# Storing V's projected memory rows by pairs of head rounds, a gate moved behind its block's projections, and another order inside a segment of a memory-recurrent attention kernel

## The chip, the cores and the metric

The kernel runs on one core of a Trainium2 chip. The metric is the time of one execution on the device in microseconds (us), the median of several. The engines are named as in the profile: PE multiplies matrices (PEld loads its weights), DVE, ACT and POOL compute on vectors, SP only issues DMAs; ACT issues DMAs too. PE writes to PSUM, and DVE or ACT copies from there to SBUF.

## The reference

Two attentions over the same x (2048 x 640, bf16) are mixed by a gate. A is a recurrence over 64 segments of 32 tokens with 8 memory tokens in front; the memory of a segment is part of the output of the one before. B is a local dilated attention. A has 32 heads of 192, so its three projections and its output projection are 640 x 6144 each.

```python
for s in range(n_seg):                       # 64 segments of 32 tokens
    h = jnp.concatenate([mem, xs], axis=1)   # 8 + 32 tokens
    q, k, v = h @ Wq, h @ Wk, h @ Wv         # per head
    scores = jnp.where(mask, q @ k.T * scale, -1e9)
    o = einsum(softmax(scores) @ v, Wo)
    mem = o[:, :M]; outs.append(o[:, M:])
g = sigmoid((x * gate_w).sum(-1))
return g * a + (1 - g) * b
```

## The kernel before, in words

The kernel has four stages. **Part B** (`part_b`) computes the local attention in blocks of 512 tokens, the gate and the transposed x. Its order per engine is set by a scheduler that starts from the order of the program. **The prepass** (`prepass`) computes q, k and v of the last 8 tokens of each segment for all 64 segments at once and stores them in DRAM, as zqk and zv. **The recurrence** (`part_a`) then needs, per segment, the projections of the 32 rows (8 memory, 24 tokens) in `hT`, and loads the other 8 tokens' rows from DRAM. **Part z** makes the outputs of those last 8 tokens after the recurrence. From the prepass on, each engine does its instructions in exactly the order of the program.

The 32 heads are taken in four rounds R of 8 (a round is a slice of 1536 columns), and the rounds in two halves h. A weight slice is 128 x 1536 bf16, 384 KB; there are 80, of which 67 lie in SBUF and 13 are streamed from DRAM in each segment, through four buffers `wst`, by SP (`load_slice`, L401 for the input weights, L400 for copies of Wo). SP issues a streamed load once its buffer is free.

One segment goes, on PE: `m_qk(0, ...)` (L580) projects q and k of the first half into the first two of four PSUM bank pairs, `m_qk(1, ...)` those of the second half into the other two; `m_qk`'s argument lists the chunks of 128 of the model width, and the last chunk is followed by `copy_pair` (L588), one copy on ACT (0.80 us) and one on DVE (0.96 us). `t_qk(h)` transposes a half (twelve 128 x 128 transposes, L607, three at a time, to the bank pairs that the copies have just read) and copies the result (L610 on DVE, L611 on ACT). `s_a`, `s_b` make the scores (L626, L635), `e_exp` the exponentials (L643, ACT) and two masks (L646, L648, DVE), `e_sum` the sums (L653, L655, PE) and their reciprocals (ACT), `e_norm` multiplies; `m_v` projects v, `pv_half` (L682, L686) multiplies with v, `o_group` (L716) is the output projection, `sel` (L729) and `tail` (L808) make the next memory and the output. In the first half, before: chunk 0 of `m_qk(1)`, `t_qk(0)`, the load of zv (`load_vz`, L566, ACT's queue), chunks 1 and 2, the scores and exponentials, chunks 3 and 4, `m_v(0, (0, 1))`, the loads of a4 (L759) and hT (L559) on ACT's queue, `t_qk(1)`, `e_sum(0)`.

V's prepass takes the rounds in the order 1, 3, 2, 0. In a round, four tiles of 128 rows (16 segments x 8 tokens) are projected (15 matmuls, L492) into one of two PSUM tiles, copied by ACT and DVE in turn (L80, L82) into one of four buffers of `zv4`, and stored by four DMAs of SP (L499), one for each of the four head groups j, in runs of 384 elements (768 bytes). Between the rounds stand loads of weights: `begin` (streamed slices ahead of time) and `load_late` (L415, slices that stay, into space that has become free). The rows of a segment's zv are the keys in the order j, round, token; `maskB`, built by POOL in `build_sel` (L522, L525, L528), says which of these keys belong to a query's round.

In part B, `make_xT(b)` transposes a block of x (L172), then computes the block's gate: twenty matmuls of one column (L183) with the gate's weight gw, an exponential on ACT (L186), three small operations on DVE (L187 to L189); then POOL makes the copies xh and zT (L193, L194, L197). `make_v` (L222) and `proj` (L235) follow, and a loop over 40 steps of scores, values and outputs. The loads are issued in the order x, mem, wv, the raw q and k weights, gw (L146).

Of the kernel before, what the change touches and what calls it, by code (L numbers as in the profile page):

```python
# [7 lines left out]
ACT = mybir.ActivationFunctionType  # L8
ALU = mybir.AluOpType
AX = mybir.AxisListType  # L10
BF = mybir.dt.bfloat16
F32 = mybir.dt.float32
# [33 lines left out]
class _K:  # L46
# [51 lines left out]
    def part_b(self):  # L98

        nc, tc, KC, S = self.nc, self.tc, self.KC, self.S  # L100
        NQ, HALO = 121, 14
# [9 lines left out]
        with ExitStack() as ctx:  # L111
# [55 lines left out]
            def make_xT(b):  # L167
# [11 lines left out]
                ps_g = bank(F32, "ps_g")  # L179
                for i in range(4):  # L180
                    c0 = HALO + t0 + 128 * i
                    for kc in range(KC):
                        nc.tensor.matmul(ps_g[:, i:i + 1], lhsT=xT[:, kc, c0:c0 + 128], rhs=gw[:, kc, :],  # L183
                                         start=(kc == 0), stop=(kc == KC - 1), skip_group_check=True)
                gs = slice(4 * b, 4 * b + 4)
                nc.scalar.activation(gz[:, gs], ps_g[:, 0:4], ACT.Exp, scale=-1.0)  # L186
                nc.vector.tensor_scalar_add(gz[:, gs], gz[:, gs], 1.0)  # L187
                nc.vector.reciprocal(self.g_sb[:, gs], gz[:, gs])
                nc.vector.tensor_scalar(out=self.omg_sb[:, gs], in0=self.g_sb[:, gs], scalar1=-1.0, scalar2=1.0,  # L189
                                        op0=ALU.mult, op1=ALU.add)  # L190
# [12 lines left out]
            nc.vector.tensor_copy(self.memT[:], ps[:, 0:8 * KC].rearrange("p (c i) -> p c i", i=8))  # L203

# [103 lines left out]
            proj(*steps[0])  # L308
            nc.gpsimd.memset(wop[:], 0.0)
# [4 lines left out]
            for i, (b, g) in enumerate(steps):  # L314
                if g == 2 and b + 1 < S // 512:
                    make_xT(b + 1)
                if (b, g) == (S // 512 - 1, 0):
# [111 lines left out]
    def prepass(self):  # L429
# [3 lines left out]
        NZ = nseg * 8  # L433
# [10 lines left out]
        with tc.tile_pool(name="pre_ps", bufs=1, space=bass.MemoryType.PSUM, reuse_waits="tile") as psp:  # L444
            n = 1
            for m in "qk":
                for R in range(4):
                    ZS2 = zs2[:, R // 2, :].rearrange("p (s f) -> p s f", f=192)
                    ZS = ZS2[:, :, 96 * (R % 2):96 * (R % 2) + 96]
                    if (m, R) == ("k", 2):  # L450
                        self.begin(*streamed("k", 2, 3), *streamed("v", 1), *streamed("v", 3)[0:1])
# [3 lines left out]
                    for t in range(3):  # L455
# [9 lines left out]
                        else:  # L465
                            dst = ZS.rearrange("p s (i c) -> p s i c", c=12)[:, :, :, 4 * t:4 * t + 4]
# [6 lines left out]
            for x, R in enumerate((1, 3, 2, 0)):  # L473
                sls = [self.get_slice(("v", R, kc)) for kc in range(KC)]
                if x == 1:
                    self.begin(*streamed("v", 2))
                if x == 2:
# [5 lines left out]
                    self.begin(*streamed("k", 0, 1))  # L483
                if x == 3:
                    self.begin(*streamed("k", 2, 3))
                for st in range(NZ // 128):
                    i = 4 * x + st
                    ZV = zv4[:, 1536 * (i % 4):1536 * (i % 4) + 1536]
                    ps = psp.tile([128, 4, NZ], F32, name=f"ps_pre{n % 2}")
                    for kc in range(KC):  # L490
                        for g in range(3):
                            nc.tensor.matmul(ps[:, g, :], lhsT=zT[:, kc, 128 * st:128 * st + 128],  # L492
                                             rhs=sls[kc][:, 512 * g:512 * g + 512], start=(kc == 0),
                                             stop=(kc == KC - 1))
                    self.evac(ZV.rearrange("p (g f) -> p g f", g=3), ps[:, 0:3, :], "act" if n % 2 else "dve")
                    n += 1
                    dst = self.zv_dram[16 * st:16 * st + 16].rearrange("s (j r i) f -> s j r i f", j=4, r=4)
                    for j in range(4):
                        nc.sync.dma_start(dst[:, j, R], ZV[:, 384 * j:384 * j + 384])  # L499
# [433 lines left out]
```

## Time and profile before

| | |
|---|---|
| time, median of 3 runs (lowest to highest) | 1759.71 us (1758.57 to 1762.41) |
| the profiled execution | 1759.71 us, of which the span from first to last instruction 1758.0 us |
| instructions | 80093 |
| PE busy | 1624.2 us, 92% of the span |
| ACT, DVE, POOL busy | 685.7, 641.9, 31.9 us |
| DMA | 434.53 MB, mean 247 GB/s |
| mean granted PE clock | 0.988 |

In the profile's lines, L12 is line 12 of the kernel. A line of a timeline has the start in us from the span's start, the length in us, the engine, the line, the operation, what it writes <- reads, the shapes and the count of merged instructions; brackets hold the idle time of the engine before it and what ended it. SPq and ACTq are the sequencers of SP and ACT, which issue the DMAs. `ps_d_5092` and `ps_d_5093` are the PSUM bank pairs of the first half, `ps_d_5090` and `ps_d_5091` those of the second; `zv_4165` is zv4, `zs_4166` the buffer zs2. A busy PE isn't PE at its peak, since the ends of matmuls are modelled; the starts are what the steps below are read from.

### The profile page before, as it was taken

Reading aid. Unit: us, or ns where it says so; the run is one execution under the profiler, and the core shown is the slowest. Engines: PE = TensorE matmul, PEld = TensorE weight load, DVE = VectorE, ACT = ScalarE, POOL = GpSimd, SP = SyncE. Lnnn points to the kernel's source line nnn. Section 1 sums busy time; section 2 is a strip of 40 time slices with the busy share of each in tenths; the row PEclk is TensorE's granted clock in tenths of the full one; section 3 lists DMA queues with packets and bytes.
Section 4 is the critical chain, followed back from the end, with each engine's and each line's share of the span. In section 5 each row is a group of like instructions: output and inputs, shape, how many; then the busy total and the mean of one; then the engine's idle time right before and its main releaser. Section 6 shows DMA issues by size and latency. Waiting matters only on the chain.

```text
span 1758.0 us, 80093 instructions
## 1 busy us (share of the span) xinstructions
PE 1624.2 (92%) x42085; PEld 751.7 (43%) x30693; DVE 641.9 (37%) x1542; ACT 685.7 (39%) x1372; POOL 31.9 (2%) x70
## 2 busy tenths in 40 slices
PE   7998999977999999999999999999999999999989
PEld 4555544433334334434444334444434444344447
DVE  4655522223333333333333333333333333333321
ACT  4766622213333333333343333443333443334340
POOL 5100000000000000000000000000000000000000
PEclk9999999989999999999999999999999999999989
DMA  9310195878888888898888988988988998989881
GB/s 331 82 29 17 42 309 142 230 228 272 282 280 278 281 280 280 278 297 274 281 286 276 285 272 274 290 284 281 292 273 280 293 286 273 294 282 290 278 269 31
DMA packets 264299, 434.53 MB, mean 247 GB/s; under 512 B 88845, under 2 KB 149781, under 8 KB 263957
## 3 DMA queue, kind: packets, MB, share of 16 engines
q1 hardware_dynamic: 172744, 378.52, 67.1%
q10 hardware_dynamic: 91212, 50.87, 10.6%
q8 instruction: 285, 4.67, 1.0%
q14 instruction: 58, 0.47, 0.1%
HBM read 395.62 MB, written 34.86 MB: 245 GB/s over the span
## 4 chain that ended last, share of the span: by engine, by line
PE 67%; DMA 10%; ACT 8%; DVE 7%; issue 4%; SPq 2%; ACTq 1%; DVEq 0%
PE ps_d_5093 L580 9%; PE ps_d_5091 L580 9%; DVE ZQKV L588 6%; DMA wst<-in_A_Wv_dram 6%; PE ps_d_5092 L716 6%; PE ps_d_5093 L716 6%; PE ps_d_5092 L580 6%; PE ps_d_5090 L580 5%; PE ps_bqk L235 3%; ACT ZQKV L693 3%; ACT bP L258 2%; PE ps_d_5093 L865 2%; PE ps_d_5093 L607 2%; PE ps_d_5091 L607 1%; PE ps_d_5091 L865 1%
## 5 line engine op out<-in xcount | busy, mean ns | idle before, releaser
L580 PEld LDWEIGHTS <-hT 128*32 128x32 bf16 x5632 | 155.3, 96 | 342.1 <-issue 258.2
L588 DVE CAST ZQKV<-ps_d_5093 128x768 bf16<-128x768 f32 x128 | 122.6, 958 | 206.3 <-PE ps_d_5093 L580 206.3
L716 PEld LDWEIGHTS <-ZQKV 128*32 128x32 bf16 x4608 | 124.2, 96 | 115.4 <-ACT ZQKV L693 55.6
L607 PEld LDWEIGHTS <-ZQKV 128*128 128x128 bf16 x1536 | 91.5, 98 | 123.5 <-ACT ZQKV L588 84.5
L716 PE MATMUL ps_d_5093<-zs_4166,ZQKV 128*32 128x384 bf16 x1792 | 140.0, 330 | 2.2 <-issue 2.2
L716 PE MATMUL ps_d_5092<-zs_4166,ZQKV 128*32 128x256 bf16 x2304 | 131.6, 277 | 7.7 <-issue 2.3
L588 ACT CAST ZQKV<-ps_d_5092 128x768 bf16<-128x768 f32 x64 | 51.2, 800 | 188.1 <-PE ps_d_5092 L580 188.1
L580 PE MATMUL ps_d_5091<-wst,hT 128*32 128x384 bf16 x1280 | 109.1, 329 | 7.5 <-DMA wst<-in_A_Wv_dram 3.1
L580 PE MATMUL ps_d_5093<-wst,hT 128*32 128x384 bf16 x1024 | 89.2, 328 | 15.2 <-DMA wst<-in_A_Wv_dram 14.7
L611 ACT COPY ZQKV<-ps_d_5091 128x768 bf16<-128x768 bf16 x64 | 51.1, 799 | 85.7 <-PE ps_d_5091 L607 81.1
L611 ACT COPY ZQKV<-ps_d_5093 128x768 bf16<-128x768 bf16 x64 | 51.1, 799 | 83.3 <-PE ps_d_5093 L607 83.3
L693 DVE CAST ZQKV<-ps_d_5091 128x384 bf16<-128x384 f32 x64 | 35.7, 558 | 117.6 <-PE ps_d_5091 L686 117.6
L626 PEld LDWEIGHTS <-ZQKV 128*32 128x32 bf16 (+1 forms) x4096 | 50.2, 92 | 65.2 <-ACT ZQKV L611 50.7
L716 PE MATMUL ps_d_5093<-zv_4165,ZQKV 128*32 128x384 bf16 x1024 | 71.9, 325 | 6.1 <-issue 5.9
L588 DVE CAST ZQKV<-ps_d_5091 128x768 bf16<-128x768 f32 x64 | 61.3, 958 | 38.8 <-PE ps_d_5091 L580 38.8
L646 DVE TENSOR_TENSOR ZQKV<-ZQKV,maskA 128x160 bf16<-128x160 bf16 x128 | 30.6, 239 | 122.6 <-ACT ZQKV L643 122.6
L716 PE MATMUL ps_d_5092<-wst,ZQKV 128*32 128x256 bf16 x768 | 71.8, 278 | 2.2 <-issue 2.2
L588 ACT CAST ZQKV<-ps_d_5090 128x768 bf16<-128x768 f32 x64 | 51.2, 799 | 45.7 <-PE ps_d_5090 L580 44.8
L258 ACT ACTIVATE bP<-ps_bS 128x968 bf16<-128x968 f32 (+1 forms) x80 | 64.7, 855 | 4.6 <-PE ps_bS L253 3.8
L682 PEld LDWEIGHTS <-ZQKV 32*128 32x128 bf16 (+1 forms) x4096 | 43.1, 97 | 49.7 <-ACT ZQKV L588 24.4
L693 ACT CAST ZQKV<-ps_d_5090 128x384 bf16<-128x384 f32 x64 | 30.7, 479 | 82.2 <-PE ps_d_5091 L686 79.9
L693 DVE CAST ZQKV<-ps_d_5093 128x384 bf16<-128x384 f32 x64 | 35.7, 558 | 67.9 <-PE ps_d_5093 L686 67.9
(639 smaller groups left out, 3849.8 us busy)
## 6 DMA issues: line engine op xcount, KB each, us to landing
wst<-in_A_Wk_dram SPq DMA_DIRECT2D x260, 384.0 KB
wst<-in_A_Wv_dram SPq DMA_DIRECT2D x260, 384.0 KB
wst<-wscr SPq DMA_DIRECT2D x192, 384.0 KB
wst<-in_A_Wq_dram SPq DMA_DIRECT2D x130, 384.0 KB
zqk_dram<-zs_4166 ACTq DMA_DIRECT2D x4, 3072.0 KB
ZQKV<-zqk_dram ACTq DMA_DIRECT2D x64, 192.0 KB
zv_dram<-zv_4165 SPq DMA_DIRECT2D x64, 96.0 KB
ZQKV<-zv_dram ACTq DMA_DIRECT2D x64, 96.0 KB
```

The costliest lines, as they stand in the source:

```text
L235: nc.tensor.matmul(ps[:, 0:nn], lhsT=wqk[n][:, kc, 4 * g:4 * g + 4, :].rearrange("p h d -> p (h d)"), rhs=xT[:, kc, o0:o0 + nn], start=(kc ...
L258: nc.scalar.activation(Pv, ps[0:nk, :, 0:nq * nu], ACT.Exp, scale=scale_b)
L580: mm = nc.tensor.matmul(dst[x // 2][32 * j:32 * j + 32, x % 2, 0:384], lhsT=hT[:, kc, :], rhs=sl[:, 384 * j:384 * j + 384], start=(kc == 0 ...
L588: cp(KV[:, 384 * u:384 * u + 768].rearrange("p (a f) -> p a f", a=2), ps[:, :, 0:384])
L607: nc.tensor.transpose(p[:, r, t, :], unit[2 * r + m][:, 128 * t:128 * t + 128], self.ident[:])
L611: nc.scalar.copy(KV[:, 4 * 384:6 * 384].rearrange("p (c b i) -> p c b i", b=4, i=8), blocks(pk))
L626: nc.tensor.matmul(pSs[h][32 * j:32 * j + 32, par, 40 * r:40 * r + 40], lhsT=KT[R][k0:k1, c, :], rhs=q_blocks(R)[k0:k1, :, c, :], start=(r ...
L646: nc.vector.tensor_tensor(out=EA, in0=EA, in1=self.maskA[:].unsqueeze(1).unsqueeze(1).to_broadcast([128, 2, 2, 40]), op=ALU.mult)
L682: nc.tensor.matmul(out[:, r, t, :], lhsT=V[2 * h + r][ks, f0:f1], rhs=E[ks, par, 40 * r:40 * r + 40], start=(r == 0 and t == 0), stop=Fals ...
L693: cp(oTxs[2 * h + jp].rearrange("p (j c) q -> p j c q", j=2), src[:, :, :, 8:40])
L716: mm = nc.tensor.matmul(b_out[part][32 * jj:32 * jj + 32, 0:n], lhsT=oTxs[2 * (R // 2) + j // 2][:, 6 * (j % 2) + 3 * (R % 2) + t, :], rhs ...
L865: nc.tensor.matmul(ps[32 * q:32 * q + 32, 0:nf], lhsT=oz[n, q][:, 24 * (R // 2) + 6 * j + 3 * (R % 2) + t, :], rhs=wo[part, c // nc_][:, c ...
```

## The change

Three things are changed.

*Part B.* The gate moves out of `make_xT` into a function `make_g`. For block 0 it is called behind `make_v(0)` and the first `proj`, for the others right behind `make_xT`, where it was, but with POOL's copies ahead of it in the program.

*The prepass.* V's rounds are taken in pairs, (0, 1) and then (2, 3). For a tile of rows both rounds are projected, copied into one of two buffers of twice the size, and stored by four DMAs with runs of 768 elements (1536 bytes): 32 DMAs in place of 64. For this the keys of a pair are interleaved (j, pair, token, round), k's in the same manner, and `maskB` is built for that order, with one select by POOL in place of three per head group, and seven additions and a copy on DVE. The loads between the rounds move to the two pairs.

*The segment.* `m_qk(1)` does chunks 0 and 1 before `t_qk(0)`, and 2, 3 and 4 behind it, all of them before the first half's scores.

```diff
@@ part_b: the gate's lines move from make_xT to a function of their own @@
+            def make_g(b):
+                t0 = 512 * b
                 ps_g = bank(F32, "ps_g")
...
             make_v(0)
             proj(*steps[0])
+            make_g(0)
             nc.gpsimd.memset(wop[:], 0.0)
...
                     make_xT(b + 1)
+                    make_g(b + 1)
@@ prepass, k's part @@
-                        self.begin(*streamed("k", 2, 3), *streamed("v", 1), *streamed("v", 3)[0:1])
+                        self.begin(*streamed("k", 2, 3), *streamed("v", 1))
...
-                            dst = ZS.rearrange("p s (i c) -> p s i c", c=12)[:, :, :, 4 * t:4 * t + 4]
+                            dst = ZS2.rearrange("p s (i r c) -> p s i r c", r=2, c=12)[:, :, :, R % 2, 4 * t:4 * t + 4]
@@ prepass, v's part @@
-            for x, R in enumerate((1, 3, 2, 0)):
-                sls = [self.get_slice(("v", R, kc)) for kc in range(KC)]
-                if x == 1:
-                    self.begin(*streamed("v", 2))
-                if x == 2:
+            for rp in range(2):
+                Rs = (2 * rp, 2 * rp + 1)
+                sls = {R: [self.get_slice(("v", R, kc)) for kc in range(KC)] for R in Rs}
+                if rp == 0:
+                    self.begin(*streamed("v", 2), *streamed("v", 3))
+                else:
                     self.load_late(2, slices(zs2[:, 1, :]))
                     nc.scalar.dma_start(self.ZQKV[:, 608:1376], self.zqk_dram[0])
...
-                    self.begin(*streamed("k", 0, 1))
-                if x == 3:
-                    self.begin(*streamed("k", 2, 3))
+                    self.begin(*streamed("k", 0, 1)[0:2])
                 for st in range(NZ // 128):
-                    i = 4 * x + st
-                    ZV = zv4[:, 1536 * (i % 4):1536 * (i % 4) + 1536]
...
+                    ZV = zv4[:, 3072 * (st % 2):3072 * (st % 2) + 3072].rearrange("p (j r f) -> p j r f", j=4, r=2)
+                    for R in Rs:
+                        ps = psp.tile([128, 4, NZ], F32, name=f"ps_pre{n % 2}")
...
+                        self.evac(ZV[:, :, R % 2, :], ps[:].rearrange("p g n -> p (g n)")[:, 0:1536].rearrange(
+                            "p (j f) -> p j f", j=4), "act" if n % 2 else "dve")
+                        n += 1
+                    if (rp, st) == (1, NZ // 128 - 1):
+                        self.begin(*streamed("k", 0, 1)[2:3], *streamed("k", 2, 3))
+                    dst = self.zv_dram[16 * st:16 * st + 16].rearrange("s (j a i r) f -> s j a i (r f)", j=4, a=2, r=2)
                     for j in range(4):
-                        nc.sync.dma_start(dst[:, j, R], ZV[:, 384 * j:384 * j + 384])
+                        nc.sync.dma_start(dst[:, j, rp], ZV[:, j].rearrange("p r f -> p (r f)"))
@@ build_sel @@
-            mb = self.maskB[sl, :, :]
...
+            nc.gpsimd.affine_select(out=self.maskB[sl, :, 0:8].rearrange("p (a r) i -> p a r i", r=2),
+                                    in_=ones[sl, 0:32].rearrange("p (a r i) -> p a r i", a=2, r=2),
+                                    pattern=[[-16, 2], [-1, 2], [-2, 8]], compare_op=ALU.is_equal, fill=0.0, base=0,
                                     channel_multiplier=1)
...
+        for q in range(1, 8):
+            nc.vector.tensor_add(self.maskB[:, :, q], self.maskB[:, :, q - 1], self.maskB[:, :, q])
+        nc.vector.tensor_copy(self.maskB[:, :, 8:16], self.maskB[:, :, 7:8].to_broadcast([128, 4, 8]))
@@ part_a, one segment @@
-                m_qk(1, (0,))
+                m_qk(1, (0, 1))
                 t_qk(0)
                 load_vz(s)
-                m_qk(1, (1, 2))
+                m_qk(1, (2, 3, 4))
                 for chunks in (FULL, HALF):
                     s_a(0, chunks)
                     s_a(1, chunks)
                     s_b(0, chunks)
                 e_exp(0)
-                m_qk(1, (3, 4))
                 if s == 0:
                     self.load_late(3, self.last_tiles)
                 m_v(0, (0, 1))
```

## The prediction

> **What bounds the kernel.** I read the page first, then the busy time by stage, then the order of work on PE, DVE and SP in one segment and in the V prepass. The page's chain of waits is mostly matmuls:
>
> ```profile
> PE 67%; DMA 10%; ACT 8%; DVE 7%; issue 4%; SPq 2%; ACTq 1%; DVEq 0%
> ```
>
> PE holds two thirds of the chain, so time is won only where PE stands still. By stage (start:end, length, busy time of each engine, granted clock, DMA share, GB/s):
>
> ```profile
> 0.00:223.00 223.00, 193.98 (x2729) 114.73 (x2729) 117.65 (x227) 142.20 (x256) 31.93 (x70) 0.98 0.31 99
> 327.00:392.00 65.00, 54.28 (x242) 23.85 (x241) 16.53 (x10) 11.51 (x8) 0.00 (x0) 0.92 0.85 233
> 392.00:421.00 29.00, 21.07 (x576) 8.87 (x393) 6.92 (x18) 7.78 (x17) 0.00 (x0) 0.88 0.83 252
> 421.00:1692.00 1271.00, 1192.08 (x36368) 511.61 (x25190) 464.57 (x1254) 487.63 (x1065) 0.00 (x0) 0.99 0.89 283
> ```
>
> The last row is 63 of the 64 segments of the recurrence, 20.2 us each; the third is the first segment, 8 us longer; the second is the V prepass, PE idle for some 11 of 65 us. All three parts of the change fall into these rows: the order inside a segment counts 64 times, the rest once.
>
> **Part 1, the order inside a segment.** The change does 32 instead of 16 matmuls between the last projection of the first half and its transposes (t_qk(0), L607), and does all of m_qk(1) before the first half's scores. PE, one segment, before:
>
> ```profile
> 1011.36 0.34 PE L580 MATMUL ps_d_5091<-wlate_k_0_4119,hT 128*32 128x384 bf16 x4
> 1011.63 0.34 PE L607 MATMUL ps_d_5092<-ident,ZQKV 128*128 128x128 bf16 x3
> 1012.15 0.33 PE L607 MATMUL ps_d_5093<-ident,ZQKV 128*128 128x128 bf16 x3 [0.18 <-DVE ZQKV L588]
> 1012.32 0.33 PE L607 MATMUL ps_d_5092<-ident,ZQKV 128*128 128x128 bf16 x3
> ...
> 1016.71 0.34 PE L607 MATMUL ps_d_5090<-ident,ZQKV 128*128 128x128 bf16 x3
> 1017.13 0.33 PE L607 MATMUL ps_d_5091<-ident,ZQKV 128*128 128x128 bf16 x3
> 1017.30 0.33 PE L607 MATMUL ps_d_5090<-ident,ZQKV 128*128 128x128 bf16 x3
> ...
> 1017.63 0.23 PE L653 MATMUL ps_d_5092<-ZQKV,bones 128*128 128x160 bf16 x1
> ```
>
> Three transposes take 0.165 us (1012.15 to 1012.32), but the second three of each half start 0.52 and 0.42 us after the first. They overwrite the bank pair that DVE is still copying:
>
> ```profile
> 1011.14 0.96 DVE L588 CAST ZQKV<-ps_d_5093 128x768 bf16<-128x768 f32 x1 [2.20 <-PE ps_d_5093 L580]
> ...
> 1015.34 0.19 DVE L648 TENSOR_TENSOR ZQKV<-ZQKV,maskB 128x64 bf16<-128x64 bf16 x1
> 1016.12 0.96 DVE L588 CAST ZQKV<-ps_d_5091 128x768 bf16<-128x768 f32 x1 [0.60 <-PE ps_d_5091 L580]
> ```
>
> The first copy ends at 1012.10 and the transposes go on at 1012.15; the second ends at 1017.08 and they go on at 1017.13. So PE loses 0.52 - 0.165 = 0.355 and 0.42 - 0.165 = 0.255, together 0.61 us a segment; the list of waits has the first 63 times.
>
> After: call T the end of m_qk(1). Eight groups of four take 1.31 us (1014.60 to 1015.91), so t_qk(0) starts 0.65 us later than now, at 1012.28, after the copy. t_qk(1) now comes behind the scores (0.55) and 16 matmuls of V (0.65, plus 0.1 to 0.15 to change over), at T+1.30. DVE's copy starts at T+0.21 and ends at T+1.17. Both waits go. Number of matmuls, loads and changes of shape: the same.
>
> What is late next is the softmax of the first half. Now its masks end at 1015.53 and the sums on PE (L653) start at 1017.63: 2.10 us of slack. The change takes from it the 1.31 us of matmuls that move ahead and the 0.255 us of the lost wait; and the masks stand behind DVE's copy, so they start at T+1.18, not at 1.13 us (1014.05 to 1015.18) after the scores' start: 0.05. That leaves 0.48 us. On ACT the copy of the first bank pair runs from T-0.06 to T+0.74, and exp could start at T+0.74 anyhow, so it isn't held. Behind exp in ACT's queue stand the loads of a4 and hT (issue 0.55 and 0.49 us), then the copy of t_qk(1)'s K (L611): they are out by about T+1.9, L611 is due at T+2.2; 0.3 us to spare. The wait that the page lists for exp, DMA ZQKV<-zv_dram in 37 segments, I don't believe: in the timeline exp starts 0.12 us after PE's last score ends. SP's streamed weights keep their order; the tightest lead, V's first slice, falls from 5.3 us (issue 1011.08, use 1016.40) to about 4.9.
>
> So 0.61 us, if nothing is given back. Something will be: DMA is at 0.89 of its time and 20.2 us become 19.6, so 0.92, and PE stalls on "issue" for 4% of the chain, 70 us or 1.1 us a segment:
>
> ```profile
> 1022.59 0.20 PE L686 MATMUL ps_d_5093<-ZQKV 32*64 32x32 bf16 x2 [1.30 <-issue]
> ```
>
> The same instructions from the first half's scores to the second half's now stand in 4.76 us (1014.05 to 1018.81) and will stand in 3.2. I let the stalls grow by a tenth, 0.11 us; the ends are nothing and a third (0.36). Net 0.50 us x 64 = **32 us** (16 to 39). The Trainium skill (Runtime: NRT & Kernel Launch, Instruction fetch mechanics) has the sequencer fetch the next block of instructions while the present one runs, a crossing "mostly hidden". By it I would give back nothing and arrive some 7 us lower; the row of 1.30 us says otherwise, if that stall is a fetch.
>
> **Part 2, V's prepass.** Its 16 tiles of 15 matmuls take 3.24 us each (333.61 to 336.85), 51.8 us; from 327.14 to 392.02 are 64.9. The rest stands in two rows of PE, and what SP did meanwhile says why:
>
> ```profile
> 381.80 1.44 PE L492 MATMUL ps_pre_5044<-wlate_v_0_4127,ZQKV 128*128 128x512 bf16 x3 [8.76 <-ACT zv_4165 L80]
> 392.02 0.35 PE L580 MATMUL ps_d_5092<-wres_q_0_71,hT 128*32 128x384 bf16 x4 [1.85 <-DVE zv_4165 L82]
> ```
> ```profile
> 362.62 7.67 SPq L415 DMA_DIRECT2D zs_4166<-in_A_Wo_dram  x8
> 370.39 3.08 SPq L401 DMA_DIRECT2D wst<-in_A_Wk_dram  x3
> 373.56 11.25 SPq L499 DMA_DIRECT2D zv_dram<-zv_4165  x16
> ```
>
> SP issues a store each 0.64 us, without a pause from 346 to 396; ACT can't empty PSUM into zv4 before the stores of the round before have landed, and PE waits 8.9 us (372.88 to 381.80), runs the next tile at half the clock (1.7 us more) and ends 2.0 us late. While SP issues the last sixteen (385 to 396) DMA is busy for 0.67: the issue is the limit, not the bytes. The change makes 32 stores of twice the size. That one takes as long to issue is not shown for stores; the weight loads, four times as large in as many rows, take 0.33 to 0.53 us to issue while the queue has room. So I take 0.64; the other end is 1.28. Half of the issues, 32 x 0.64 = 20 us, leave SP. Walked through: first pair's last stores out by 358, eight weights by 365, two streamed weights by 367, first stores of the second pair 367 to 369.6, landed some 3.3 us later (as the lane that a store of 352.35 frees at 355.68), 372.9, where tile buffer 0 is wanted at 369.5; PE loses 2 us, ends at 381 and hands over at 383 instead of 392: **9 us** (0 with 1.28 us an issue; 10 at best). The interleaved keys cost PE and DVE nothing there: the same copies in another order, masks built elsewhere.
>
> The first segment waits 1.72 us for a q and 5.86 us for a v slice, both behind the last stores in SP's queue. These end 2.6 instead of 4.0 us into the segment, with fewer packets pending: **2.5 us** (0 to 6). The Trainium skill (DMA: Bandwidth & Descriptors, Specifications) puts the shortest transfer at full rate at 512 bytes. That speaks against this part: 768 bytes are above it already, and by bytes alone I would leave out the 9 us and forecast some 9 us more. The 0.67 while SP issues decides for me.
>
> **Part 3, the gate.**
>
> ```profile
> 14.32 0.69 PE L183 MATMUL ps_g<-gw_sb,xT 128*128 128x1 bf16 x20 [5.45 <-DMA gw_sb<-in_gate_w_dram]
> 14.87 8.15 PE L222 MATMUL ps_bv<-wv_sb,xT 128*128 128x320 bf16 x40
> ```
>
> V's projections stand behind a gate that waits for its weight. x's last copy ends at 9.62; wv is issued before raws that land by 11.04; so L222 can start 3.8 to 5.2 us earlier. K's last padded weights come from POOL at 18.87, which caps the shift at 5.0 (L235 of K is at 23.89). Against it: DVE gets eight small operations (0.17 us each by L189, 1.4 us) behind POOL's selects, in front of the first score masks. The other blocks' gates stay where they are in PE's order. I take **3 us**, ends -1 and 5.
>
> **Sum.** 32 + 9 + 2.5 + 3 = 46.5 from the profiled execution's 1759.71 (span 1758.0 and 1.7 around it; it is the median run): 1713. By the ends: 1759.71 - (39 + 10 + 6 + 5) = 1700, and 1759.71 - (16 + 0 + 0 - 1) = 1745.
>
> **Rivals.** (a) The recurrence gives it all back, to DMA at 0.92 or to PE's issue stalls: parts 2 and 3 alone, 1745. For it speaks the DMA share; against it, PE waits for weights in the recurrence are 20 us in all. (b) A store of 192 KB takes twice as long to issue: 1713 + 9 = 1722. (c) Slower: the softmax's cover breaks. It decides once the first half's masks end over 0.48 us later than worked out (ACT serving its copy, exp and two DMA issues in an order that holds exp or L611); each further 0.1 us costs 6.4 us, and at a wait of 1.1 us on L653 the segment loses 0.49 net, 64 x 0.49 = 31, less 14.5: 1776. Against it: none of these rows is longer than 0.96 us.
>
> **Numbers.** Forecast 1713 with its ends: 0.61; (a) 0.16; (b) 0.10; (c) 0.10; parts that just cancel: 0.03. Range 1699 to 1746. Faster by over 0.2% (about what a measurement can tell) 0.87, within 0.03, slower 0.10.
>
> **What would show it.** Right: second three transposes 0.165 us behind the first in both halves; L653 without a DVE wait in the first half; segments of 19.6 to 19.8 us; no PE gap over 3 us in V's prepass, recurrence from about 380; L222 from 10 or 11. Wrong: a wait of L653 on L648, issue stalls well over 4%, stores over 1 us apart on SP.

## The result

The changed kernel takes 1729.59 us (median of 4 runs, 1727.93 to 1730.83) against 1759.14 for the kernel before, run beside it (4 runs, 1757.46 to 1762.41): a ratio of 0.9829, 95% interval 0.9812 to 0.9846. It is faster, inside the range, but by 29.5 us and not by 46.5. The profiled execution took 1729.13 us, its span is 1727.4. The kernel before varies from chip to chip (medians of 1750 to 1759 us below), so every ratio stands against its runs on the same chip.

The page's chain of the kernel after, and the busy time by stage (columns as before):

```profile
PE 75%; DMA 9%; ACT 8%; issue 4%; DVE 2%; ACTq 1%; SPq 1%; POOL 1%; DVEq 0%; POOLq 0%
```
```profile
0.00:229.00 229.00, 198.05 (x2729) 115.65 (x2729) 117.79 (x235) 142.26 (x256) 30.69 (x62) 0.96 0.31 96
332.00:394.00 62.00, 54.66 (x244) 24.17 (x243) 16.12 (x10) 11.50 (x8) 0.00 (x0) 0.97 0.86 246
394.00:422.00 28.00, 21.01 (x568) 8.89 (x389) 7.19 (x19) 7.40 (x17) 0.00 (x0) 0.88 0.82 253
422.00:1662.00 1240.00, 1173.72 (x36384) 512.51 (x25194) 462.13 (x1254) 487.61 (x1066) 0.00 (x0) 0.99 0.90 290
```

DVE's share of the chain fell from 7% to 2% and PE's rose from 67% to 75%: what DVE no longer holds up is the recurrence. But POOL is now in the chain, and the first stage, part B, lasts until 229 where it lasted until 223, with eight more DVE instructions (235 for 227) and a lower clock. By stretches of the two profiled executions (us, spans):

| stretch | before | after | change | forecast |
|---|---|---|---|---|
| part B, to the start of the prepass | 223.53 | 229.08 | +5.55 | -3 |
| prepass of q and k | 103.61 | 103.61 | 0 | 0 |
| prepass of V | 64.88 | 61.67 | -3.21 | -9 |
| first segment | 28.26 | 27.49 | -0.77 | -2.5 |
| the other 63 segments | 1279.26 | 1246.96 | -32.30 | -32 |
| end | 58.44 | 58.59 | +0.15 | 0 |
| sum | 1757.98 | 1727.40 | -30.58 | -46.5 |

The recurrence gave what was forecast. Half of what is missing (8.55 of 15.92 us) was lost in part B, where something cost more than the whole gate was to bring.

**One segment of the recurrence after**, PE and then DVE, around the two groups of transposes (L612, L607 before):

```profile
1016.13 0.34 PE L612 MATMUL ps_d_5060<-ident,ZQKV 128*128 128x128 bf16 x3
1016.31 0.33 PE L612 MATMUL ps_d_5061<-ident,ZQKV 128*128 128x128 bf16 x3
...
1020.18 0.34 PE L612 MATMUL ps_d_5058<-ident,ZQKV 128*128 128x128 bf16 x3
1020.36 0.33 PE L612 MATMUL ps_d_5059<-ident,ZQKV 128*128 128x128 bf16 x3
...
1020.86 0.23 PE L658 MATMUL ps_d_5060<-ZQKV,bones 128*128 128x160 bf16 x1
```
```profile
1015.00 0.96 DVE L593 CAST ZQKV<-ps_d_5061 128x768 bf16<-128x768 f32 x1 [2.20 <-PE ps_d_5061 L585]
...
1019.08 0.96 DVE L593 CAST ZQKV<-ps_d_5059 128x768 bf16<-128x768 f32 x1 [1.61 <-PE ps_d_5059 L585]
...
1020.15 0.18 DVE L653 TENSOR_TENSOR ZQKV<-ZQKV,maskB 128x64 bf16<-128x64 bf16 x1
```

In each half the second three transposes now come 0.18 us behind the first. DVE's copies end at 1015.96 and 1020.04, ahead of them. The softmax's masks end at 1020.33 and its sums (L658) start at 1020.86: the slack that I worked out as 0.48 us is 0.53. Over all segments the two groups fell from means of 1.115 and 0.924 us to 0.774 and 0.680, together 0.585; the mean segment went from 20.18 to 19.67.

**Part B after**, DVE and then PE:

```profile
22.60 0.66 DVE L82 CAST bqT<-ps_bqk 128x484 bf16<-128x484 f32 x1 [6.74 <-PE ps_bqk L238]
27.63 1.24 DVE L533 TENSOR_TENSOR maskB<-maskB 128x4 bf16<-128x4 bf16 x6 [4.37 <-POOL maskB L528]
...
29.27 0.66 DVE L82 CAST bqT<-ps_bqk 128x484 bf16<-128x484 f32 x1
```
```profile
9.40 2.85 PE L225 MATMUL ps_bv<-wv_sb,xT 128*128 128x320 bf16 x10 [0.92 <-DMA wv_sb<-in_B_wqkv_dram]
15.63 5.91 PE L225 MATMUL ps_bv<-wv_sb,xT 128*128 128x320 bf16 x30 [3.38 <-ACT bV_247 L80]
...
29.98 2.17 PE L238 MATMUL ps_bqk<-xT,wq_pad 128*128 128x484 bf16 x5 [3.11 <-DVE bqT L82]
```

The additions that build the new mask (L533) stand on DVE in front of the second bias copy (L82), and wait 4.4 us for POOL's last selection. The copy, due near 25.5 when its five matmuls (24.27, 1.18 us long) have ended, starts at 29.27; PE, which needs its PSUM bank, stands still for 3.1 us and then does five matmuls in 2.17 us that took 1.19.

### The profile page after: what moved, and what is told of

The parts are those of the page before. It is cut to its first block, busy times and chain, and to the rows that moved or that the text cites. A ratio compares the mean times of both kernels' runs of the same rounds, so it can differ in the third digit from the quotient of the medians.

```text
span 1727.4 us, 79984 instructions
## 1 busy us (share of the span) xinstructions
PE 1608.3 (93%) x42085; PEld 752.3 (44%) x30693; DVE 639.1 (37%) x1550; ACT 685.4 (40%) x1372; POOL 30.7 (2%) x62
## 4 chain that ended last, share of the span: by engine, by line
PE 75%; DMA 9%; ACT 8%; issue 4%; DVE 2%; ACTq 1%; SPq 1%; POOL 1%; DVEq 0%; POOLq 0%
PE ps_d_5061 L585 11%; PE ps_d_5059 L585 10%; PE ps_d_5060 L721 6%; PE ps_d_5061 L721 6%; PE ps_d_5058 L585 5%; PE ps_d_5060 L585 5%; DMA wst<-in_A_Wv_dram 3%; PE ps_bqk L238 3%; DMA wst<-in_A_Wq_dram 3%; ACT ZQKV L698 2%; ACT bP L261 2%; DMA wst<-in_A_Wk_dram 2%; PE ps_d_5061 L869 2%; PE ps_d_5058 L612 2%; PE ps_d_5060 L612 1%
## 5 line engine op out<-in xcount | busy, mean ns | idle before, releaser
L585 PEld LDWEIGHTS <-hT 128*32 128x32 bf16 x5632 | 157.6, 96 | 339.3 <-issue 248.7
L721 PEld LDWEIGHTS <-ZQKV 128*32 128x32 bf16 x4608 | 125.4, 96 | 117.1 <-ACT ZQKV L698 56.5
L721 PE MATMUL ps_d_5061<-zs_4166,ZQKV 128*32 128x384 bf16 x1792 | 140.4, 329 | 2.8 <-issue 2.7
L721 PE MATMUL ps_d_5060<-zs_4166,ZQKV 128*32 128x256 bf16 x2304 | 132.1, 278 | 9.0 <-issue 3.4
L612 PEld LDWEIGHTS <-ZQKV 128*128 128x128 bf16 x1536 | 86.6, 98 | 91.9 <-ACT ZQKV L593 49.0
L585 PE MATMUL ps_d_5059<-wst,hT 128*32 128x384 bf16 x1280 | 111.2, 329 | 9.7 <-DMA wst<-in_A_Wq_dram 3.7
L585 PE MATMUL ps_d_5061<-wst,hT 128*32 128x384 bf16 x1024 | 89.4, 328 | 11.0 <-DMA wst<-in_A_Wv_dram 10.9
L616 ACT COPY ZQKV<-ps_d_5061 128x768 bf16<-128x768 bf16 x64 | 51.1, 798 | 105.7 <-PE ps_d_5061 L612 105.7
L616 ACT COPY ZQKV<-ps_d_5059 128x768 bf16<-128x768 bf16 x64 | 51.1, 798 | 80.7 <-PE ps_d_5060 L660 72.8
L721 PE MATMUL ps_d_5061<-zv_4165,ZQKV 128*32 128x384 bf16 x1024 | 72.2, 326 | 3.8 <-issue 3.6
L721 PE MATMUL ps_d_5060<-wst,ZQKV 128*32 128x256 bf16 x768 | 71.9, 276 | 3.8 <-issue 3.8
L615 DVE COPY ZQKV<-ps_d_5060 128x768 bf16<-128x768 bf16 x64 | 35.7, 558 | 64.4 <-PE ps_d_5060 L612 64.4
```

Source lines behind the costliest of these rows:

```text
L585: mm = nc.tensor.matmul(dst[x // 2][32 * j:32 * j + 32, x % 2, 0:384], lhsT=hT[:, kc, :], rhs=sl[:, 384 * j:384 * j + 384], start=(kc == 0 ...
L612: nc.tensor.transpose(p[:, r, t, :], unit[2 * r + m][:, 128 * t:128 * t + 128], self.ident[:])
L615: nc.vector.tensor_copy(QTa[:, 2 - h:6 - h].rearrange("p b r c i -> p (r c) b i"), blocks(pq))
L616: nc.scalar.copy(KV[:, 4 * 384:6 * 384].rearrange("p (c b i) -> p c b i", b=4, i=8), blocks(pk))
L721: mm = nc.tensor.matmul(b_out[part][32 * jj:32 * jj + 32, 0:n], lhsT=oTxs[2 * (R // 2) + j // 2][:, 6 * (j % 2) + 3 * (R % 2) + t, :], rhs ...
```

## The experiments

Theory: the new segment order alone gives the gain; part 2 falls short because the second pair's first stores stand behind 3.9 MB of loads; part B loses to the mask chain on DVE. Rivals: the gate's new place costs the 5.5 us; the stalls that remain are PE's own supply of instructions. The times, and the stretches of each profiled run (us):

| run | median (runs' range) | ratio to before, 95% | prepass starts | prepass of V | first segment | mean segment |
|---|---|---|---|---|---|---|
| before | 1759.14 | 1 | 223.53 | 64.88 | 28.26 | 20.18 |
| after | 1729.59 | 0.9829 (0.9812 to 0.9846) | 229.08 | 61.67 | 27.49 | 19.67 |
| order_alone | 1725.41 (1721.43 to 1727.74) | 0.9857 (0.982 to 0.9894) | 221.94 | 65.91 | 27.64 | 19.63 |
| mask_later | 1726.87 (1725.00 to 1727.32) | 0.9866 (0.9824 to 0.9907) | 226.66 | 62.40 | 26.82 | 19.65 |
| stores_first | 1717.53 (1712.57 to 1720.56) | 0.9812 (0.9773 to 0.985) | 226.96 | 56.58 | 26.46 | 19.65 |
| late_v_first | 1717.57 (1716.11 to 1723.02) | 0.982 (0.9783 to 0.9858) | 226.59 | 61.81 | 25.02 | 19.57 |
| mask_prepass | 1722.64 (1713.93 to 1734.69) | 0.981 (0.9748 to 0.9872) | 228.72 | 68.39 | 26.10 | 19.66 |
| gate_back | 1728.88 (1723.84 to 1730.27) | 0.9836 (0.979 to 0.9881) | 228.15 | 61.97 | 27.04 | 19.68 |
| mask_gate | 1723.53 (1721.50 to 1731.41) | 0.9807 (0.9754 to 0.9859) | 225.24 | 61.88 | 27.34 | 19.77 |
| order_mid | 1756.01 (1743.34 to 1762.22) | 0.9983 (0.995 to 1.0017) | 228.25 | 61.94 | 27.32 | 20.19 |
| mask_pool | 1716.40 (1713.47 to 1725.41) | 0.9809 (0.9752 to 0.9866) | 219.19 | 62.31 | 26.21 | 19.58 |
| combined | 1715.70 (1706.98 to 1720.34) | 0.9782 (0.9732 to 0.9833) | 222.19 | 56.84 | 26.18 | 19.66 |
| combined_gate | 1715.86 (1710.12 to 1727.34) | 0.9797 (0.9738 to 0.9856) | 223.33 | 57.81 | 27.96 | 19.67 |
| half_new | 1660.95 (one run) | | 227.86 | 62.16 | 27.22 | 18.62 |

The first four experiments shared a chip, the next four a second one, the last four a third. Whole times resolve some 10 us at best (the recurrence of runs that are equal there differs by up to 13 us), so repairs of a few us are read from their own stretch.

### 1. The order alone

The kernel before with the segment's new order, nothing else: `m_qk(1, (0,)) / t_qk(0) / m_qk(1, (1, 2)) / scores / m_qk(1, (3, 4))` becomes `m_qk(1, (0, 1)) / t_qk(0) / m_qk(1, (2, 3, 4)) / scores`.

> The kernel before with the segment's new order alone (part 1), V's prepass, masks and gate as before. Theory (the order is worth 0.51 us a segment by itself, and parts 2 and 3 together were worth nothing): segments of 19.67 us on the mean in place of 20.18, transposes of both halves without a wait on DVE, part B's end and the recurrence's start unchanged (392.0 us), time 1727 us (1724 to 1730), so no slower than the whole change. Rival (part of the gain came from V's prepass and the first segment): segments of 19.9 us or more, 1738 us or more.

Measured: mean segment 19.63 us; part B and the prepass stay as they were before. Part 1 alone makes the gain; parts 2 and 3 together add nothing that the whole time shows.

### 2. The order half undone

```diff
-                m_qk(1, (2, 3, 4))
+                m_qk(1, (2,))
...
                 e_exp(0)
+                m_qk(1, (3, 4))
```

> The changed kernel with the segment's order half undone: two of the second half's five projection chunks still stand ahead of the first half's transposes, but the scores go back between the third chunk and the last two, ahead of the second half's transposes. Theory (each transpose group's wait is for its own copy, and the one chunk ahead of it hides it): the first group stays near 0.77 us, the second goes back to 0.92 us, the mean segment gains 0.22 to 0.28 us, that is 19.89 to 19.93 us, and the whole is 14 to 17 us longer than the changed kernel. Rival (the give-back belongs to the place of the scores, whose late exponential then holds the bank of the next half): the mean segment stays within 0.1 us of 19.67.

A miss. The segment lost not half of its gain but all of it. PE, DVE and ACT of one segment:

```profile
1007.66 0.84 PE L612 MATMUL ps_d<-ident,ZQKV 128*128 128x128 bf16 x12
...
1008.94 0.34 PE L585 MATMUL ps_d<-wlate_k,hT 128*32 128x384 bf16 x4
1009.40 0.28 PE L631 MATMUL ps_d<-ZQKV 128*32 128x40 bf16 x16
...
1012.06 1.09 PE L612 MATMUL ps_d<-ident,ZQKV 128*128 128x128 bf16 x12
```
```profile
1008.45 0.56 DVE L615 COPY ZQKV<-ps_d 128x768 bf16<-128x768 bf16 x1 [0.96 <-PE ps_d L612]
```
```profile
1008.55 0.80 ACT L616 COPY ZQKV<-ps_d 128x768 bf16<-128x768 bf16 x1 [1.60 <-PE ps_d L612]
```

The first group is as fast as in the changed kernel (0.774 us on average), the second as slow as before (0.926): so far as the theory has it. What it left out is the way from the transposes to the scores. ACT's copy of the transposed keys (L616) ends at 1009.35 and the scores start at 1009.40, though the last projection ahead of them was issued at 1008.94 and the next instruction could follow 0.16 us later. One chunk (0.65 us) between transposes and scores does not cover that copy: the way from the first of its matmuls to the first score takes 0.96 us (median), where 16 matmuls take 0.66: 0.30 lost where 0.34 was won. The five chunks have to cover three copies, and 2 + 3 with the scores behind is the one of the three orders tried that covers all of them.

### 3. The mask chain and the gate

Two kernels were to take the chain out of the way. Both move the loop of L533 and the copy behind it from the end of `build_sel` into a function of its own; mask_later calls it at the ninth step of part B, mask_prepass first of all in the prepass.

```diff
@@ mask_later, part_b @@
+                if (b, g) == (1, 0):
+                    self.finish_masks()
@@ mask_prepass, prepass @@
+            self.finish_masks()
             n = 1
```

> The whole change, with the seven additions and the copy that build maskB on DVE moved from the beginning of part B to its ninth step. Theory (part B ends 5.5 us later than before because these operations stand in DVE's queue behind POOL's selects and hold the copy of the second step's queries, after which PE runs at half its clock): DVE copies the second step's queries by 25 us, not at 29.3; the prepass starts at 222.5 to 224 us in place of 229.1; time 1722 to 1725 us against 1729.6. Rival (the moved gate is to blame, because ACT's queue is held by the loads of the next block's x while V's first projections wait): the prepass starts at 227 us or later, 1727 us or more.

> The changed kernel, with the six additions and the copy that finish the second mask moved out of the first part into the start of the prepass, where DVE keeps the order of the program, so that they now really leave the stretch around 26 us. Theory (the additions wait 4.4 us for POOL's selections in front of DVE's bias copy at 29.3 us, and PE's third step waits for that copy, then runs at half clock): prepass start 222 to 224 us against 226.6 to 229.1 of the changed kernel, the idle time ahead of the third step's first long matmul under 1 us, and some 3 to 5 us off the whole. Rival (the gate's new place, or the x loads in ACT's queue, set the loss): the prepass start stays at 226.5 or more and the whole within 1 us of the changed kernel's 1727 to 1730.

Neither tested the theory. In mask_prepass, DVE:

```profile
27.61 1.23 DVE L537 TENSOR_TENSOR maskB<-maskB 128x4 bf16<-128x4 bf16 x6 [4.39 <-POOL maskB L529]
```

The chain is where it was, at 27.61 with the same wait (in mask_later at 26.17 with 4.76). The edits changed the program's text and not DVE's queue. In mask_prepass the chain is called where each engine was said to keep exactly the order of the program, and it came back into part B all the same; that the scheduler of part B pulled it forward, because it waits for POOL's selections alone, is concluded from its place. So next to the gate, alone (gate_back) and with the edit of mask_prepass (mask_gate):

```diff
             make_xT(0)
+            make_g(0)
...
             proj(*steps[0])
-            make_g(0)
```

> The changed kernel with each block's gate back in its old place, ahead of the block's first projection; the mask chain stays where it is. Theory (mask chain): nothing regained by this, prepass start 226.5 to 232 us. Rival (the gate's new place costs the 5.5 us): prepass start 222 to 224 us and 4 to 5 us off the whole. By my forecast's price of 3 us for the gate's move, undoing it would cost 3 us: 230 to 232.

> Both of the above: the mask chain in the prepass and the gate in its old place. What the first part does is then, instruction for instruction but for one POOL selection per quarter, that of the kernel before. If the mask chain and the gate are all that lies between the two kernels there, the prepass starts at 221.9 to 223.5 us as before. Against the run with the mask chain alone moved it shows the worth of the gate's move: forecast 3 us longer with the gate in its old place; a gate that is worth nothing: the same within 0.5 us.

With the chain not moved, these two are the same kernel in part B, and their prepass starts at 228.15 and 225.24: on one chip, part B differs by 2.9 us between two executions. At the third step 1.3 us of that are there (29.95 and 28.67), and these follow POOL: its copies of the weights came at 11.68 and 14.82 us in the one, after loads that landed later, and at 11.09 and 13.61 in the other, and the chain on DVE at 27.67 and 26.39. The two runs of that chip with the gate in its new place (mask_prepass and order_mid) start the prepass at 228.72 and 228.25: undoing the gate regains 0.1 to 0.6 us in one execution and 3.0 to 3.5 in the other. So far nothing was settled.

The test that worked gives the chain to POOL, behind its own selections, so that it can't stand in DVE's queue:

```diff
-            nc.vector.tensor_add(self.maskB[:, :, q], self.maskB[:, :, q - 1], self.maskB[:, :, q])
-        nc.vector.tensor_copy(self.maskB[:, :, 8:16], ...)
+            nc.gpsimd.tensor_add(self.maskB[:, :, q], self.maskB[:, :, q - 1], self.maskB[:, :, q])
+        nc.gpsimd.tensor_copy(self.maskB[:, :, 8:16], ...)
```

> The changed kernel with the seven additions and the copy that finish the second mask given to POOL, behind its own selections, so that none of them stands in DVE's queue. In the run that was meant to move them into the prepass they still came on DVE at 27.61 us with the same 4.39 us of waiting, so that run has not tested them. Theory (mask chain in front of DVE's bias copy): the copy runs by 26 us in place of 29.3, the idle time ahead of PE's next projection falls from 3.1 to under 1 us and it runs at 1.2 us, not 2.2; prepass start 222.5 to 225 us against 226.6 to 229.1 with the chain on DVE. Rival (something else is late there: the transposed keys, the band product behind POOL's selections, the gate): another wait of 2 us or more takes its place and the prepass starts at 226.5 us or later.

DVE and PE of that run:

```profile
20.88 0.66 DVE L82 CAST bqT<-ps_bqk 128x484 bf16<-128x484 f32 x1 [6.50 <-PE ps_bqk L238]
...
23.78 0.66 DVE L82 CAST bqT<-ps_bqk 128x484 bf16<-128x484 f32 x1
```
```profile
25.09 1.20 PE L238 MATMUL ps_bqk<-xT,wq_pad 128*128 128x484 bf16 x5
```

The second copy runs 2.9 us behind the first and not 6.7, PE doesn't wait, and its five matmuls take 1.20 us. The prepass starts at 219.19 us, further ahead than expected. The price is cleanest at the start of part B's eleventh step, on the chip that ran the last four: 70.34 us with the chain on DVE (half_new, whose part B is the changed kernel's), 64.42 and 64.87 with it on POOL (mask_pool and combined). **The chain costs 5.5 to 5.9 us** there; on all chips the seven executions with the gate's new place and the chain on DVE are at 69.29 to 71.68. With it gone the gate can be read too: combined_gate, with the gate in its old place, is at 66.02, so **the gate's move brings some 1.2 to 1.6 us**, under a loss four times as large. This size rests on one execution against two, and gate_back and mask_gate, the same there, are 3.1 us apart at this step (70.86 and 67.75). The sign is firmer: the three executions without the chain and with the old place (66.02, 66.19 for the kernel before, 67.16 for order_alone) all lie above the two with the new one.

### 4. The prepass of V: stores ahead of loads

The second pair's eight late loads go behind its first four stores:

```diff
                 else:
-                    self.load_late(2, slices(zs2[:, 1, :]))
...
                         nc.sync.dma_start(dst[:, j, rp], ZV[:, j].rearrange("p r f -> p (r f)"))
+                    if (rp, st) == (1, 0):
+                        self.load_late(2, slices(zs2[:, 1, :]))
```

> The whole change, with the eight loads of load_late(2) issued behind the first tile's stores of the second pair, not ahead of them. Theory (PE's stop of 4.3 us and the slow tile after it come from stores that stand behind 3.9 MB of loads in one queue): no PE gap over 1 us in the second pair, recurrence from 388 us in place of 394.4, the first segment takes back up to 3 us since the same bytes come later; 1724 to 1727 us. Rival (the stores are limited by the rate at which SP issues): the stop stays at 3 us or more and the time at 1729 us.

SP and ACT of the changed kernel, then SP of this one:

```profile
341.19 23.57 SPq L506 DMA_DIRECT2D zv_dram<-zv_4165  x16
364.80 6.77 SPq L420 DMA_DIRECT2D zs_4166<-in_A_Wo_dram  x8
371.67 1.54 SPq L406 DMA_DIRECT2D wst<-in_A_Wk_dram  x2
373.31 13.72 SPq L506 DMA_DIRECT2D zv_dram<-zv_4165  x12
```
```profile
382.70 1.44 ACT L80 CAST zv_4165<-ps_pre_4974 128x1536 bf16<-128x1536 f32 x1 [11.05 <-DMA zv_dram<-zv_4165]
```
```profile
363.19 1.04 SPq L406 DMA_DIRECT2D wst<-in_A_Wk_dram  x2
367.10 2.47 SPq L505 DMA_DIRECT2D zv_dram<-zv  x4
369.61 6.57 SPq L420 DMA_DIRECT2D zs<-in_A_Wo_dram  x8
```

In the changed kernel the second pair's first stores leave SP from 373.31 on, behind ten loads of 384 KB (3.9 MB), and free the buffer for ACT at 382.70, some 7.5 us after the fourth was issued (375.17). Moved ahead of the eight late loads, they leave 36.5 us into V's prepass instead of 40.6; PE's wait of 4.34 us at 384.19 is gone, the granted clock of the stretch is 1.00 for 0.97, and V's prepass takes 56.58 us against 61.7 to 62.4 in the runs without the edit (68.39 in one, see below). Four stores of 192 KB in 2.47 us is 0.62 us each: the bytes doubled, the issue time did not grow.

### 5. The first segment's late loads

```diff
-                if s == 0:
-                    self.load_late(3, self.last_tiles)
                 m_v(0, (0, 1))
...
                 m_v(0, (2, 3, 4))
+                if s == 0:
+                    self.load_late(3, self.last_tiles)
```

> The whole change, with the four loads of load_late(3) behind the first two v slices of the first segment, not ahead of them. Theory (the first segment waits 5.8 us for a v slice because four loads of 384 KB are ahead of it in SP's queue): the first segment takes 22 to 23.5 us in place of 27.5, time 1725 us. Rival (DMA is full there whatever the order; the wait moves to the slices that are now later): 26 us or more, 1728 to 1730 us.

Partly. The first segment takes 25.02 us instead of 26.8 (the same chip's run without the edit): PE's wait for the V slice falls from the 5.83 us of the changed kernel to 1.45, but an issue stall of 2.24 us stands in front of it. In the two combined kernels, which have the same edit, V's wait was 3.19 and 4.26 us and the first segment took 26.18 and 27.96. It gains 2 us or nothing; these runs don't settle it.

### 6. Three repairs together

combined has the edits of mask_pool, stores_first and late_v_first; combined_gate that of gate_back as well.

> The changed kernel with three repairs together: the mask chain on POOL, the second pair's late loads behind its first four stores, the first segment's late V slices behind the first two. If each gives what it should by its own stretch (part B 3 to 5 us, V prepass 5 us, first segment 1 to 2.5 us) and they do not meet: prepass start 222.5 to 225, V prepass 56 to 58 us long, first segment 24.5 to 26.5 us, 9 to 12 us off the changed kernel, ratio to the kernel before 0.973 to 0.979.

> The same with the gate in its old place. With the chain on DVE the gate's old place gave a prepass start of 225.2 and 228.2 us, its new one 226.6 to 229.1. With the chain gone: by my forecast (the gate's move is worth 3 us) the prepass starts 3 us later than in the run beside it; if the move only exchanges one wait for another, within 1 us of it; if its new place itself costs, 1 us or more earlier.

Part B and V's prepass kept their gains (prepass from 222.19, V's prepass 56.84 us); the first segment shows none (26.18 us, and 26.21 in mask_pool without that edit). The sum is not resolved: 1715.70 us, ratio 0.9782 (0.9732 to 0.9833), against 0.9809 (0.9752 to 0.9866) for the mask chain alone beside it. It is the fastest median of the kernels that load all their weights, and faster than the kernel before; that it beats the changed kernel is likely from the stretches, while the ratios' intervals touch. The gate's old place started the prepass 1.1 us later than in combined and 4.1 later than in mask_pool. The part B of these two is the same and they differ by 3.0 us, so the start of the prepass doesn't tell the 3 us of the forecast from less; the eleventh step above does it better.

### 7. What the remaining stalls are

From the second segment on:

```diff
+        if pool is self.wstream and self.half:
+            h = t.rearrange("p (a f) -> p a f", a=2)[:, 0, :]
+            return t, lambda: self.nc.sync.dma_start(h, src[:, 0:768])
```

> The changed kernel with every streamed weight slice cut to half its columns from the second segment on: the other half of each streamed slice keeps what an earlier load left, so that part of the projections and of the output step is computed from old weights; instructions and their order are the same, the streamed bytes are halved. A segment of the changed kernel takes 19.67 us where the sum of its parts' shortest times is 17.85, so 1.8 us are stalls in scattered places. Theory (they are loads that land late, under the streamed traffic): with half the bytes the stalls fall to 0.3 to 0.9 us, segment 18.2 to 18.8. Rival (PE's own instruction supply): segment stays at 19.4 or more.

The recurrence of the changed kernel with half of the streamed bytes, and the page's chain:

```profile
422.00:1592.00 1170.00, 1148.75 (x36282) 500.26 (x25109) 460.72 (x1253) 485.63 (x1062) 0.00 (x0) 1.00 0.61 170
```
```profile
PE 83%; ACT 9%; DMA 3%; issue 2%; DVE 2%; POOL 1%; SPq 0%; ACTq 0%; DVEq 0%; POOLq 0%
```

DMA's share falls from 0.90 to 0.61 and the segment from 19.67 to 18.62 us: 1.05 of the 1.8 us go with the bytes. The size is the theory's, and the rival in its form (19.4 or more whatever the bytes) is out. The theory's cause is not what the rows show. The page calls "issue" the time in which an engine waited for nothing that the profile shows. PE's costliest such waits in the recurrence, before the colon the line, behind it us in total, times and longest, of the changed kernel and then with half of the bytes (L735 is L721, L599 is L585, and its rows join all bank pairs):

```profile
PE ps_d_5060 L721 <- issue: 7.2, 11, 1.6
PE ps_d_5059 L585 <- issue: 5.7, 8, 1.2
```
```profile
PE ps_d L735 <- issue: 3.4, 9, 0.6
PE ps_d L599 <- issue: 0.8, 2, 0.5
```

Over segments 2 to 63 and all lines, PE's waits of more than 0.15 us fall from 40.6 to 4.5 us where they are "issue" and from 7.2 to nothing where a load was late. So of the 65 us regained there, 36 had no visible cause, though the instructions are the same, and only 7 were loads that land late; the rest is in gaps too short for this count. This fits a supply of instructions that suffers from the load on DMA, but no run shows that these waits are fetches. The instruction queue's packets (16 KB) took 1.05 us each in the recurrence with the full bytes and 1.08 with half, so they don't move faster; whether they start sooner was not tried.

## Why the prediction was right, and where it was not

**Part 1, right in mechanism and size.** Forecast 0.61 us of waits removed, 0.11 given back, 32 us. Measured 0.585 removed (0.341 and 0.244 for 0.355 and 0.255), 0.51 a segment, so 0.08 given back: 32.3 us. The 0.08 is not resolved: the mean segment of this order is 19.57 to 19.77 us over the runs with the full bytes. PE's "issue" waits went from 33.8 to 40.6 us in the profiled pair (0.11 a segment), but they are 32.2 to 44.3 in the other runs. Only the first group's copy, the second's and the softmax were walked through; order_mid showed a fourth wait, that of the scores for the transposed keys, which three chunks happen to cover. Rivals (a) and (c) did not happen: no sum waits for a mask. The Trainium skill (Runtime: NRT & Kernel Launch, Instruction fetch mechanics) has the crossing to the next block of instructions mostly hidden; by that nothing would have been given back. The 0.08 is near it, but if the issue waits are fetches, how much is hidden depends here on DMA's load: 40.6 us at a share of 0.90, 4.5 at 0.61.

**Part 2, mis-sized: 3.2 us for 9.** Rival (b) is out: a store of 192 KB is issued in 0.62 us while the queue has room; those that take about 1 us or more stand behind bulk loads, as those of 96 KB did. The step that failed is the landing in "first stores of the second pair 367 to 369.6, landed some 3.3 us later". The issue came as walked through: the whole prepass of V started 5.55 us later, and counted from its start the four stores were to go out from 39.9 to 42.5 us and went out from 40.6 to 43.1. But they freed the buffer some 7.5 us after the fourth was begun, not 3.3: that figure was of a store with few loads ahead of it, this one had 3.9 MB. The kernel before has a nearer row. ACT waits there for the first four of the sixteen stores that follow eleven loads, and the fourth was begun at 375.42, so 4.9 us:

```profile
380.30 1.44 ACT L80 CAST zv_4165<-ps_pre_5002 128x1536 bf16<-128x1536 f32 x1 [15.46 <-DMA zv_dram<-zv_4165]
```

PE lost 4.3 us for the 2 of the forecast and, at about half its speed, 1.7 more; 1.5 us in the first pair (at 353.79) were not in the walk either. With the stores ahead of the loads the stretch gives 8.3 us, and 9.3 against order_alone, which has the old prepass on the same chip: the forecast's 9. This fits SP's issue as the limit before, as argued, and the queue once it was gone. That the gain comes from fewer stores and not from their longer runs is argued from SP's rows; no run has one without the other. So the Trainium skill's shortest transfer at full rate, 512 bytes (DMA: Bandwidth & Descriptors, Specifications), by which nothing was to come, is neither borne out nor refuted.

**The first segment, 0.8 us for 2.5.** V's wait of 5.83 us is as long as before (5.86): the late loads still go out ahead of the V slice. The step "These end 2.6 instead of 4.0 us into the segment" came out better than forecast, 1.2 us (the last two stores from 394.37, 1.18 us), and V waited all the same. So it is not the stores that it stands behind. Moving the late loads behind it shortened the wait to 1.45 us in one kernel, but in the two combined ones to 3.19 and 4.26, where stores_first has 4.17 without that edit: what sets it stays open.

**Part 3, wrong: 5.5 us lost for 3 won.** The gate's move was half as good (some 1.2 to 1.6 us). V's projections did start early, at 9.4, but stopped after ten matmuls: ACT, which empties their PSUM, was issuing three x loads for 6.4 us and came back at 15.15; it did so for 4.6 us in the kernel before. That ACT's queue was not looked at is the smaller error. The larger is the step "DVE gets eight small operations (0.17 us each by L189, 1.4 us) behind POOL's selects, in front of the first score masks". Duration and predecessor were right. Not priced was the wait itself (4.4 us on DVE, by which the bias copy came 3.8 us late), and what stood behind it was not the score masks but, ahead of them, the bias copy for which PE waits. The step also named POOL's selections without asking when they end (27.59 us, behind a 4.36 us fill). The effect, 5.5 to 5.9 us, lies beyond the end of -1 that I gave the part; less the gate's gain it makes 3.9 to 4.7, and the rest of the 5.55 is within the 3 us by which part B varies. The total is inside its range all the same because part 1, right, is two thirds of it, and the ends of all parts were added up; the 46.5 itself was missed by more than a third.

## What to carry to other kernels

When an edit adds instructions to an in-order queue, price the moment at which their last input is ready and list what stands behind them there; the sum of their durations is the smallest part. A reordering needs each copy on its path checked against the work that covers it: an order that hides one wait can open another of the same size, as the half-undone order did. And a store that frees a buffer belongs ahead of bulk loads in the same queue; see on the engine's own timeline that an edit has moved what it was meant to move.

## What was not expected of the hardware

- A PE idle time of about 3 us can be paid twice, but its length alone doesn't decide. In V's prepass the next 18 matmuls took 4.04 us after 2.74 us and less. They ran at about half that speed for a while after 3.09 us, and in all eleven cases from 3.79 us on; after 3.30 us in combined_gate they ran at full speed. In part B, after 2.21 us in order_mid, five matmuls ran at full speed and the five behind them at about half. In mask_prepass two waits, of 3.09 and 5.70 us, make V's prepass 68.39 us at a clock of 0.90 where the same code took 61.7 to 62.4. The rows are of mask_prepass, combined_gate and order_mid:

```profile
355.01 6.90 PE L497 MATMUL ps_pre<-wlate_v,ZQKV 128*128 128x512 bf16 x18 [3.09 <-ACT zv L80]
```
```profile
349.83 4.04 PE L495 MATMUL ps_pre<-wlate_v,ZQKV 128*128 128x512 bf16 x18 [3.30 <-ACT zv L80]
```
```profile
31.45 1.18 PE L238 MATMUL ps_bqk<-xT,wq_pad 128*128 128x484 bf16 x5 [2.21 <-DVE bqT L82]
32.47 2.10 PE L238 MATMUL ps_bqk<-xT,wk_pad 128*128 128x498 bf16 x5
```

- The issue of a store of 128 rows by SP took 0.56 to 0.66 us at 96 KB and at 192 KB, and about 1 to 1.7 us at both sizes where bulk loads stood ahead: it does not depend on the bytes here.
- Part B, the same instructions on the same chip, varies by some 3 us from execution to execution (225.24 and 228.15, 219.19 and 222.19). In the first pair 1.3 us come from when loads of weights land; the rest was not looked into.
